# K^T and V^T by transposing DMAs in place of TensorE transposes, in an attention and GLU training step on one core

## The chip, the cores and the metric

The kernel runs on one core of a Trainium2 chip. The metric is the device time of one execution in microseconds (us). A core has TensorE (PE; its weight loads are shown as PEld), VectorE (DVE), ScalarE (ACT), GpSimd (POOL) and SyncE (SP), which work side by side and wait for one another by semaphores; DMA engines move data for the queues that SP and POOL issue.

## What is computed

The reference is a forward pass and its gradients for eight inputs. With S = 2048 rows, D = 576, H = 32 heads of 128 and F = 4608, all in bf16:

```python
xn = layernorm(x)
s  = attention(xn @ wq, k_cache, v_cache) @ wo   # 32 heads, softmax over 2048 keys
g  = silu(glu(xn, w_gate, w_up, w_down))         # (sigmoid(xn@w_gate) * (xn@w_up)) @ w_down
out = x + s * g
# out, and the gradients for x, k_cache, v_cache, wq, wo, w_gate, w_up, w_down
```

## The kernel before, in words

The kernel goes through stages: layer norm and the GLU forward (up to about 510 us of the profile), attention forward and backward for 32 heads (513 to 3774 us), and then the output, the GLU's gradients and the gradient for x. The change lies in the attention stage alone.

**One head.** K and V of a head come from DRAM as natural tiles Kn and Vn, 128 partitions x 16 blocks x 128 (L390, L392, queue of POOL; Kn has two buffers, Vn one). The head's Q^T and dO^T are projections on TensorE. The score matmuls need K^T, and the dP matmuls V^T, each 128 x 2048: TensorE transposes the 16 blocks of Kn, and of Vn, in two groups of eight into PSUM (L431), and VectorE copies each group to KT or VT (L42). KT and VT have one buffer each. For each of the 16 query tiles (128 rows) the first half of the head makes the scores (L465), their scaled negative with a running minimum on VectorE (sneg, L467), the exponentials Pq on ScalarE (L476), and P^T by a transposing DMA of SP (PT, L513), from which TensorE sums the output row by row with Vn (L525). The second half makes dP (L495), dS on VectorE and ScalarE (dSq, L498 to L505), dS^T by a transposing DMA (dST, L513; for query tile 9 alone by TensorE), and dQ rows with Kn (L525). The gradients for V and K (L544) take Pq and dSq as they are, and run beside the rows of the same and of the next head.

**The order is written by hand.** Every piece of a head has a position on a scale of 64 per head: query tile qt has its scores at 2 qt and 2 qt + 1, its dP at 32 + 2 qt and 33 + 2 qt. The other pieces are given with `at(position, function, ...)`: PT is issued at 2 qt + 2.7, dST at 32 + 2 qt + 2.0, the rows are summed from 12.1 positions after the scores (or dP) on. `back(x)` is position x of the head before. K^T of the next head stands at 46.3 and 48.3 of this head, V^T at 22.2 and 24.2 of its own. All entries are sorted by position and called in that order. Inside `tc.manual_schedule(engines=MAN)` the engines of MAN (PE, DVE, ACT) run in the order in which the code calls them; for the others, SP and POOL, a scheduler sets the order. In either case an engine works through its own list in order, so an instruction that waits holds up those behind it.

SP's list in this stage: 16 PT and 15 dST per head, 31 transposing DMAs of 128 x 2048 bf16 (512 KB), and in the last head five loads of Wo into tiles that are no longer needed (L374) and then the loads of oT for the next stage (L694). PT and dST share a pool of seven buffers; Pq and dSq share one of twenty.

Of the kernel before, what the change touches and what calls it, by code (L numbers as in the profile page):

```python
# [9 lines left out]
bf = mybir.dt.bfloat16  # L10
# [3 lines left out]
P = 128  # L14
# [81 lines left out]
def kernel(  # L96
# [6 lines left out]
    nc = tc.nc  # L103
    cfg = dict(cfg or {})
    _, S, D = A_x.shape
# [232 lines left out]
    with tc.tile_pool(name="ld2", bufs=2) as ld2, tc.tile_pool(name="ld1q", bufs=1) as ld1q, \  # L338
# [17 lines left out]
        def at(pos, fn, *args):  # L356
            prog.append((pos, len(prog), fn, args))

        def anchor(pos, fn, *args):
            anchors.append((pos, len(anchors), fn, args))  # L360
# [67 lines left out]
        def pe_transposes(src_fn, dst, g, eng):  # L428
            pt = ps_acc.tile([P, 8, P], bf, name="acct", tag="acc")
            for j in range(8):  # L430
                nc.tensor.transpose(pt[:, j, :], src_fn(g * 8 + j), ident[:])  # L431
            alt.copy(dst[:, g * 8:(g + 1) * 8, :], pt[:], eng=eng)

        def prep_kt(hs, g, eng):
            if g == 0:
                hs.KT = ld1.tile([P, S], bf, name="KT")
            pe_transposes(lambda j: hs.Kn[:, j, :], hs.KT[:].rearrange("p (t q) -> p t q", q=P), g, eng)

        def prep_vt(hs, g, eng):
            if g == 0:  # L440
                hs.VT = ld1.tile([P, S], bf, name="VT")
            pe_transposes(lambda j: hs.Vn[:, j, :], hs.VT[:].rearrange("p (t q) -> p t q", q=P), g, eng)

        def prep_don(hs, g, eng):
            if g == 0:
# [84 lines left out]
        def rows(pos, step, width, hs, T, rhs, g, sinks):  # L530
            bx = Box()
            sink, after = sinks
            for j in range(GQ):
                for kt in range(NT):
                    at(pos + step * j + width * kt / NT, row_mm, bx, hs, T, rhs, g * GQ + j, kt, sink)
            if after:
                at(pos + step * (GQ - 1) + width + AFTER, after)
# [11 lines left out]
        def kv(pos, end, hs, slabs, rhs, half, out_dram):  # L549
            ov = out_dram.rearrange("(p t) d -> p t d", t=NT)  # L550
            bx = Box()
            bx.acc = [None, None]

            def sink(acc, i):
                c = half * 2 + i
                kv_t = stg.tile([P, KPC, P], bf, name="kv")
                alt.copy(kv_t[:], acc[:], eng=KVE[i])
                nc.gpsimd.dma_start(ov[:, c * KPC:(c + 1) * KPC, :], kv_t[:])

            n = 2 * KPC  # L560
            for qt in range(NT):
                for j in range(n):
                    at(pos + (end - pos) * (qt * n + j) / (NT * n), kv_mm, bx, hs, slabs, rhs, half, qt, j, sink)

        def o_sink(hs, g):
            gs = slice(g * GQ, (g + 1) * GQ)
            bx = Box()

            def sink(acc):
                bx.ou = wt.tile([P, GQ, P], bf, name="ou")  # L570
                alt.copy(bx.ou[:], acc[:], eng=OUE)
                bx.prod = wt.tile([P, GQ, P], f32, name="prod", bufs=1)
                nc.gpsimd.tensor_tensor(bx.prod[:], bx.ou[:], hs.dOn[:, gs, :], op=ALU.mult)

            def after():
                prod, ou = bx.prod, bx.ou
                o_n = stg.tile([P, GQ, P], bf, name="o_n", bufs=1)
                nc.vector.tensor_reduce(hs.delta[:, gs], prod[:], axis=AX.X, op=ALU.add)
                nc.gpsimd.tensor_scalar(hs.negdelta[:, gs], hs.delta[:, gs], -1.0, None, op0=ALU.mult)
                nc.gpsimd.tensor_tensor(o_n[:], ou[:], bcast(hs.rinv_all[:, gs], GQ), op=ALU.mult)  # L580
                nc.gpsimd.dma_start(on2_d[g * CH:(g + 1) * CH, hs.h * P:(hs.h + 1) * P].rearrange("(t p) d -> p t d", p=P), o_n[:])

            return sink, after

        def dq_sink(hs, g):
            gs = slice(g * GQ, (g + 1) * GQ)

            def sink(acc):
                dq_n = stg.tile([P, GQ, P], bf, name="dq_n")
                nc.vector.tensor_tensor(dq_n[:], acc[:], bcast(hs.rsc[:, gs], GQ), op=ALU.mult)  # L590
                nc.gpsimd.dma_start(dq2_d[g * CH:(g + 1) * CH, hs.h * P:(hs.h + 1) * P].rearrange("(t p) d -> p t d", p=P), dq_n[:])  # L591

            return sink, None
# [3 lines left out]
        XO, XQ = 12.1, 12.1  # L597
        VA, VB, KA, KB = (22, 38.0), (38.5, 53.5), (58.0, 69.5), (70.5, 82.0)
        QP, DO, KVE, PJE, OUE = (41.0, 3.0), (4.0, 2.5), "ss", "sv", "s"
        KT_AT, DON_AT, VT_AT, QN_AT = (46.3, 2, "v"), (7.2, 5, "v"), (22.2, 2, "v"), (38.3, 2, "s")  # L600
        EXP_AT, RINV_AT, PT_AT, DST_AT, AFTER = 2.1, 4.6, 2.7, 2.0, 3.5
        WO_AT = 50.0
        MAN = {mybir.EngineType.PE, mybir.EngineType.DVE, mybir.EngineType.Activation}
        for h in range(H):
            hs = Head(h)
            b = h * HEAD
            back = lambda x: b - HEAD + x if h else b - 14 + x / 8
            at(back(35.0), load_w, hs)
            at(back(35.1), load_kv, hs)
            for c in range(NCH):  # L610
                at(back(QP[0] + QP[1] * c), proj, hs, "QT", c, PJE[0])
                at(b + DO[0] + DO[1] * c, proj, hs, "dOT", c, PJE[1])
            at(b + DO[0] - 2, prep_wo, hs, "s")
            for g in range(2):
                at(back(KT_AT[0] + KT_AT[1] * g), prep_kt, hs, g, KT_AT[2])
                at(b + DON_AT[0] + DON_AT[1] * g, prep_don, hs, g, DON_AT[2])
                at(b + VT_AT[0] + VT_AT[1] * g, prep_vt, hs, g, VT_AT[2])
                at(b + QN_AT[0] + QN_AT[1] * g, prep_qn, hs, g, QN_AT[2])
            for p in range(NT // 2):
                at(b + 4 * p + 2 + RINV_AT, s_rinv, hs, p)  # L620
                at(b + max(4 * p + 2.1 + RINV_AT, DON_AT[0] + DON_AT[1] * (p // 4) + 0.5), s_scale, hs, p)
            for qt in range(NT):
                p1, p2 = b + 2 * qt, b + H1 + 2 * qt
                for hf in range(NHF):
                    anchor(p1 + hf, s_half, hs, qt, hf)
                    anchor(p2 + hf, dp_half, hs, qt, hf)
                at(p1 + EXP_AT, s_exp, hs, qt)
                if qt in PE_P:
                    for g in range(2):
                        at(p1 + 5.3 + g, trans_pe, hs.PT, hs.P, qt, "PT", g, "s")  # L630
                else:
                    at(p1 + PT_AT, trans_dma, hs.PT, hs.P, qt, "PT")
                if qt in PE_DS:
                    for g in range(2):
                        at(p2 + 4.3 + g, trans_pe, hs.dST, hs.dS, qt, "dST", g, "sv"[g])
                else:
                    at(p2 + DST_AT, trans_dma, hs.dST, hs.dS, qt, "dST")
            for g in range(NG):
                rows(b + 8 * g + XO, 2, 2, hs, hs.PT, "Vn", g, o_sink(hs, g))
                rows(b + H1 + 8 * g + XQ, 2, 2, hs, hs.dST, "Kn", g, dq_sink(hs, g))  # L640
            for half, (pv, pk_) in enumerate(((VA, KA), (VB, KB))):
                kv(b + pv[0], b + pv[1], hs, hs.P, "dOn", half, out_3[0, h])
                kv(b + pk_[0], b + pk_[1], hs, hs.dS, "Qn", half, out_2[0, h])
# [4 lines left out]
                at(bl + WO_AT + 3 * k, load_wo, h0, min(h1, H - 1))  # L648
        prog.sort(key=lambda e: e[:2])
        anchors.sort(key=lambda e: e[:2])  # L650
        with tc.manual_schedule(engines=MAN):
            nxt = 0
            for (pos, _, fn, args) in prog:
                while nxt < len(anchors) and anchors[nxt][0] <= pos:
                    anchors[nxt][2](*anchors[nxt][3])
                    nxt += 1
                fn(*args)

    OB = 5
    if True:  # L660
# [19 lines left out]
        with tc.tile_pool(name="c1b", bufs=1, side="right", reuse_waits="tile") as blk, \  # L680
# [3 lines left out]
                tc.tile_pool(name="c1pt", bufs=2, space=PSUM) as pst, \  # L684
                tc.manual_schedule(engines=MAN | {mybir.EngineType.SP, mybir.EngineType.Pool}):
            gins = {}
# [188 lines left out]
        with tc.tile_pool(name="c4c", bufs=1, reuse_waits="tile") as chp, tc.tile_pool(name="c4s", bufs=2, reuse_waits="tile") as sb, \  # L875
# [10 lines left out]
            for sbi in range(S // SB2):  # L886
# [20 lines left out]
                for sl in range(nsl):  # L907
# [17 lines left out]
                    t = sb.tile([P, D], f32, name="t")  # L925
# [38 lines left out]
```

## Time and profile before

| | |
|---|---|
| median of three runs (lowest, highest) | 5231.35 us (5222.84, 5238.27) |
| span of the profiled execution | 5231.1 us |
| attention, first to last head's score start (31 heads) | 517.3 to 3640.0 us, 100.7 us a head |
| TensorE, share of the span | 97%, mean granted clock 0.996 |
| VectorE, ScalarE, GpSimd | 62%, 44%, 28% |
| copies PSUM to KT, 64 | 691 ns each |
| copies PSUM to VT, 64 | 686 ns each |
| transposing DMAs PT and dST | 512 and 480, median 5.9 us from issue to landing |

The profile is one execution. A page of it has the busy time of each engine, the span in 40 slices with the busy share in tenths, the DMA queues, the chain of work that ended last, and the groups of instructions with busy time, mean duration, idle time before them and what ended it. A matmul's duration runs from issue to the modelled end of a pipeline, so neighbouring matmuls overlap, and the pace is read from the starts. A slice of SP's queue holds the wait of the instruction as well as its issue; the transfer itself comes after it, up to the landing.

### The profile page before, as it was taken

What the parts mean: (1) busy time and instruction counts of PE and PEld (TensorE: products, weight loads), DVE (VectorE), ACT (ScalarE), POOL (GpSimd) and SP (SyncE); (2) the same over time, 40 slices, a digit from 0 to 9 for tenths busy, and PEclk for the clock granted to TensorE, in tenths of its full rate; (3) what the DMA queues carried; (4) which work ended last, traced back from release to release, by engine and by line L of the source; (5) the groups of instructions that cost most, each with busy time, mean ns of one, the idle gap of its engine ahead of it and who ended that gap; (6) DMA issues with size and microseconds to landing.
All of it is one profiled execution on the core that took longest, in us unless ns stands there. A gap on an engine that the chain in (4) does not pass through costs nothing.

```text
span 5231.1 us, 128038 instructions
## 1 busy us (share of the span) xinstructions
PE 5100.0 (97%) x55184; PEld 3649.0 (70%) x55184; DVE 3262.9 (62%) x5108; ACT 2290.1 (44%) x2931; POOL 1444.3 (28%) x2102
## 2 busy tenths in 40 slices
PE   8999999999999999999999999999899999999999
PEld 3444777777777777777777777777657788744454
DVE  4545888888888888888888888888532222210111
ACT  6531665565566556556556655655301221100000
POOL 2222233233233323323323332332222222211000
PEclk9999999999999999999999999999999999999999
DMA  7489999999999999999999999999999556686765
GB/s 274 183 205 166 190 192 199 193 197 194 193 197 198 198 198 199 199 197 195 197 202 198 194 201 199 197 197 201 204 223 227 174 169 185 200 232 152 162 146 124
DMA packets 2712232, 1013.46 MB, mean 194 GB/s; under 512 B 2525296, under 2 KB 2645872, under 8 KB 2711664
## 3 DMA queue, kind: packets, MB, share of 16 engines
q1 hardware_dynamic: 2628256, 726.57, 80.8%
q0 software_dynamic: 83408, 278.71, 17.9%
q8 instruction: 431, 7.06, 0.6%
q14 instruction: 137, 1.12, 0.1%
HBM read 172.54 MB, written 201.00 MB: 71 GB/s over the span
## 4 chain that ended last, share of the span: by engine, by line
PE 81%; issue 6%; DVE 6%; DMA 5%; POOL 1%; SPq 1%; ACT 0%; DVEq 0%; POOLq 0%; ACTq 0%
PE acckv L544 15%; PE acc L525 14%; PE dp L495 8%; PE acc L905 7%; PE sp L465 6%; PE accw L807 6%; DVE sneg L467 4%; PE accp L424 4%; PE dh L781 3%; PE acc L306 3%; PE accd L795 3%; PE accq L863 3%; PE acc L854 2%; PE acct L431 2%; PE acc L723 2%
## 5 line engine op out<-in xcount | busy, mean ns | idle before, releaser
L476 ACT ACTIVATE Pq<-sneg,nm 128x2048 bf16<-128x2048 bf16 x512 | 1024.5, 2001 | 389.2 <-DVE sneg L467 386.1
L525 PE MATMUL acc<-Kn,dST 128*128 128x128 bf16 x8192 | 1066.6, 219 | 22.5 <-DMA dST<-dSq 22.4
L525 PE MATMUL acc<-Vn,PT 128*128 128x128 bf16 x8192 | 1022.4, 219 | 10.7 <-DMA PT<-Pq 10.7
L544 PE MATMUL acckv<-dOn,Pq 128*128 128x128 bf16 x8192 | 1031.7, 219 | 0.0
L498 DVE SCALAR_TENSOR_TENSOR dSq<-dp,delta,Pq 128x1024 bf16<-128x1024 f32 x608 | 773.6, 1281 | 349.9 <-PE dp L495 347.6
L544 PE MATMUL acckv<-Qn,dSq 128*128 128x128 bf16 x8192 | 896.2, 219 | 0.0
L544 PEld LDWEIGHTS <-Pq 128*128 128x128 bf16 x8192 | 793.3, 98 | 117.1 <-issue 0.3
L525 PEld LDWEIGHTS <-PT 128*128 128x128 bf16 x8192 | 765.8, 98 | 153.2 <-DMA PT<-Pq 14.2
L525 PEld LDWEIGHTS <-dST 128*128 128x128 bf16 x8192 | 759.0, 98 | 158.1 <-DMA dST<-dSq 28.8
L544 PEld LDWEIGHTS <-dSq 128*128 128x128 bf16 x8192 | 719.0, 98 | 99.8 <-issue 0.3
L467 DVE TENSOR_SCALAR_CACHE_REDUCE sneg<-sp,nm 128x1024 bf16<-128x1024 f32 x512 | 656.5, 1282 | 82.0 <-PE sp L465 56.5
L467 DVE TENSOR_SCALAR_CACHE_REDUCE sneg<-sp 128x1024 bf16<-128x1024 f32 x512 | 625.0, 1221 | 59.5 <-PE sp L465 51.2
L501 ACT ACTIVATE t<-dp,negdelta 128x1024 bf16<-128x1024 f32 x416 | 463.6, 1114 | 420.1 <-PE dp L495 363.2
L465 PE MATMUL sp<-KT,QT 128*128 128x512 bf16 x2048 | 609.2, 379 | 32.5 <-DVE sneg L467 25.4
L495 PE MATMUL dp<-VT,dOT 128*128 128x512 bf16 x2048 | 609.5, 379 | 0.3 <-DVE dSq L498 0.3
L484 POOL TENSOR_TENSOR dOn<-dOn,rinv_all 128x256 bf16<-128x256 bf16 x256 | 155.9, 609 | 658.0 <-DVE rinv_all L480 540.9
L505 DVE TENSOR_TENSOR dSq<-t,Pq 128x1024 bf16<-128x1024 bf16 x416 | 319.0, 767 | 0.0
L807 PEld LDWEIGHTS <-xn_all 128*128 128x128 bf16 (+1 forms) x2880 | 282.7, 100 | 38.6 <-issue 11.1
L905 PEld LDWEIGHTS <-cf 128*128 128x128 bf16 x2304 | 146.0, 98 | 141.7 <-DMA cf<-dg_d 3.6
L918 DVE SCALAR_TENSOR_TENSOR junk<-dxn,xn_all 128x576 f32<-128x576 f32 x16 | 12.1, 758 | 370.3 <-ACT dxn L913 370.3
L591 POOL DMA_DIRECT2D dq_d<-dq_n x128 | 98.6, 770 | 471.9 <-DVE dq_n L590 463.5
L465 PEld LDWEIGHTS <-QT 128*128 128x128 bf16 x2048 | 163.3, 98 | 53.1 <-issue 51.7
(173 smaller groups left out, 6956.1 us busy)
## 6 DMA issues: line engine op xcount, KB each, us to landing
out_dram<-kv POOLq DMA_DIRECT2D x256, 128.0 KB, 4.8
h_d<-h_row POOLq DMA_DIRECT2D x48, 384.0 KB, 2.7
a_d<-a_row POOLq DMA_DIRECT2D x48, 384.0 KB, 2.6
b_d<-b_row POOLq DMA_DIRECT2D x48, 384.0 KB, 3.2
a_blk<-a_d SPq DMA_DIRECT2D x18, 1024.0 KB, 5.8
b_blk<-b_d SPq DMA_DIRECT2D x18, 1024.0 KB, 21.3
du_d<-du_blk POOLq DMA_DIRECT2D x18, 1024.0 KB, 8.5
dg_d<-dg_blk POOLq DMA_DIRECT2D x18, 1024.0 KB, 11.5
```

The costliest lines, as they stand in the source:

```text
L424: nc.tensor.matmul(acc[:], lhsT=w[:, i, :], rhs=srcT[:, i, cs], start=(i == 0), stop=False)
L465: nc.tensor.matmul(sp[:, c * CH:(c + 1) * CH], lhsT=hs.QT[:, qs], rhs=hs.KT[:, hf * HW_ + c * CH: hf * HW_ + (c + 1) * CH], start=True, st ...
L467: nc.vector.tensor_scalar(sneg[:, hf * HW_:(hf + 1) * HW_], sp[:], -SCALE, None if hf == 0 else nm[:, hf - 1:hf], op0=ALU.mult, op1=ALU.mi ...
L476: nc.scalar.activation(Pq[:], sneg[:], AF.Exp, bias=nm[:, hf:hf + 1], scale=-1.0, accum_out=hs.rs_all[:, qt:qt + 1])
L495: nc.tensor.matmul(dp[:, c * CH:(c + 1) * CH], lhsT=hs.dOT[:, qs], rhs=hs.VT[:, hf * HW_ + c * CH: hf * HW_ + (c + 1) * CH], start=True, s ...
L498: nc.vector.scalar_tensor_tensor(dSq[:, hsl], dp[:], hs.delta[:, qt:qt + 1], Pq[:, hsl], op0=ALU.subtract, op1=ALU.mult)
L501: nc.scalar.activation(t[:], dp[:], AF.Identity, bias=hs.negdelta[:, qt:qt + 1], scale=1.0)
L505: nc.vector.tensor_tensor(dSq[:, hsl], t[:], Pq[:, hsl], op=ALU.mult)
L525: nc.tensor.matmul(bx.acc[:, j, :], lhsT=T[qt][:, kt, :], rhs=getattr(hs, rhs)[:, kt, :], start=(kt == 0), stop=(kt == NT - 1))
L544: nc.tensor.matmul(bx.acc[i][:, jj, :], lhsT=slabs[qt][:, k0:k0 + P], rhs=getattr(hs, rhs)[:, qt, :], start=(qt == 0 and jj == 0), stop=(q ...
L807: nc.tensor.matmul(acc[:kd, :FB], lhsT=xn_all[:, st, d0:d0 + kd], rhs=blk_[:, st, :], start=(st == 0), stop=(st == NT - 1))
L905: nc.tensor.matmul(accs[sl][j][:, :nn], lhsT=ch[:, kk, sl * P:(sl + 1) * P], rhs=w_[:, n0:n0 + nn], start=(pi == 0 and kk == 0), stop=(las ...
```

## The change

The eight-block groups of TensorE transposes of Kn and Vn with their copies (`prep_kt`, `prep_vt`) are replaced by one transposing DMA each, issued by SP from the natural tile (`turn`). V^T moves from positions 22.2 and 24.2 to 5.6 of its head, K^T from 46.3 and 48.3 to 52.4 of the head before. SP joins the engines that run in the written order in this stage.

```diff
-        def prep_kt(hs, g, eng):
-            if g == 0:
-                hs.KT = ld1.tile([P, S], bf, name="KT")
-            pe_transposes(lambda j: hs.Kn[:, j, :], hs.KT[:].rearrange("p (t q) -> p t q", q=P), g, eng)
-
-        def prep_vt(hs, g, eng):
-            if g == 0:
-                hs.VT = ld1.tile([P, S], bf, name="VT")
-            pe_transposes(lambda j: hs.Vn[:, j, :], hs.VT[:].rearrange("p (t q) -> p t q", q=P), g, eng)
+        def turn(hs, name, src):
+            t_ = ld1.tile([P, S], bf, name=name)
+            setattr(hs, name, t_)
+            nc.sync.dma_start_transpose(t_[:].rearrange("p (t q) -> p t q", q=P), src(hs).rearrange("p t d -> p (t d)"))
...
-        KT_AT, DON_AT, VT_AT, QN_AT = (46.3, 2, "v"), (7.2, 5, "v"), (22.2, 2, "v"), (38.3, 2, "s")
+        KT_AT, DON_AT, VT_AT, QN_AT = 52.4, (7.2, 5, "v"), 5.6, (38.3, 2, "s")
...
         MAN = {mybir.EngineType.PE, mybir.EngineType.DVE, mybir.EngineType.Activation}
+        MANH = MAN | {mybir.EngineType.SP}
...
+            at(b + VT_AT, turn, hs, "VT", lambda hs: hs.Vn[:])
+            at(back(KT_AT), turn, hs, "KT", lambda hs: hs.Kn[:])
             for g in range(2):
-                at(back(KT_AT[0] + KT_AT[1] * g), prep_kt, hs, g, KT_AT[2])
                 at(b + DON_AT[0] + DON_AT[1] * g, prep_don, hs, g, DON_AT[2])
-                at(b + VT_AT[0] + VT_AT[1] * g, prep_vt, hs, g, VT_AT[2])
...
-        with tc.manual_schedule(engines=MAN):
+        with tc.manual_schedule(engines=MANH):
```

## The prediction

> **What bounds the kernel now.** I read the page first (busy time, the 40 slices), then one head of the attention stage by itself (windows, TensorE's groups, the chain), then TensorE's waits over 26 heads, then the SP queue and the DMA.
>
> ```profile
> PE 5100.0 (97%) x55184; PEld 3649.0 (70%) x55184; DVE 3262.9 (62%) x5108; ACT 2290.1 (44%) x2931; POOL 1444.3 (28%) x2102
> PEclk9999999999999999999999999999999999999999
> DMA  7489999999999999999999999999999556686765
> ```
>
> TensorE (PE) is busy 97% of the span at the full granted clock, but so are the DMA engines in nearly every slice of the attention stage (slices 4 to 29), and the change moves work from the first to the second. "Busy" is no proof of a bound for either, so I take one head: its first score matmul (L465) starts at 2032.0 us, the next head's at 2132.6, so a head is 100.6 us. Its two halves, then TensorE's waits between 1000 and 3600 us (25.8 heads):
>
> ```profile
> 2032.00:2082.20 50.20, 49.00 (x630) 38.59 (x627) 45.17 (x80) 33.05 (x36) 14.36 (x22) 1.00 1.15 197
> 2082.20:2132.60 50.40, 50.40 (x656) 40.03 (x654) 39.38 (x47) 26.52 (x30) 18.36 (x25) 1.00 1.16 203
> ```
>
> ```profile
> PE sp L465 <- DVE sneg L467: 17.2, 51, 0.4
> PE acc L525 <- DMA dST<-dSq: 9.7, 10, 1.6
> PE acct L431 <- DVE dq_n L590: 5.8, 26, 0.2
> PE acc L525 <- DMA PT<-Pq: 1.7, 5, 0.8
> ```
>
> The columns of a window are length, busy time of PE, PEld, DVE, ACT, POOL, clock, DMA share, GB/s. TensorE idles 1.2 us in the first half and not at all in the second; all its waits in 2600 us are 34.4 us. So **attention runs at TensorE's pace**, and what leaves its list shortens the head by its own length, unless something else is nearly as long. VectorE is: 45.2 of 50.2 us in the first half, and the chain of this head runs through it there (L467, 2065 to 2075 us). The DMA share of 1.15 means that packets overlap, so it doesn't tell how full the engines are.
>
> **The change, part by part.**
>
> *TensorE loses 32 transposes a head.* The chain of this head shows what eight cost when nothing waits:
>
> ```profile
> 2045.10 0.45 PE acct L431 x8
> 2110.55 0.45 PE acct L431 x8
> ```
>
> 0.45 us for eight is 56 ns each (the row's "219 ns" is a pipelined duration, three of which overlap). Four groups a head: 1.8 us. 32 heads: 128 x 0.45 = **57.6 us off**. Beside the row: the Trainium skill, "VectorE: DVE Perf Modes", section "The three transpose paths", gives 390 ns for such a block on TensorE and 1309 ns by DMA, and its rule is to use TensorE where a PSUM destination will do, so it speaks against this change. By its figure 1024 transposes would free an estimated 399 us of TensorE; the trace has a seventh of that.
>
> *VectorE loses four copies a head.* The row of VT's copies has 686 ns, that of KT's 691: 1.37 + 1.38 = 2.75 us a head. In the second half VectorE is off the path (39.4 of 50.4). In the first half the two V^T copies stand at positions 22 and 24 of the head's 64 (1.57 us each, so 2066 to 2071 us), where the chain is on VectorE. There it loses 1.37 us against TensorE's 0.9, 0.47 us more slack a head. The waits of the scores for sneg are put down by their place in the head from TensorE's starts: 22 us of lost time over all 32 heads fall on the score tiles 11 to 13, behind these copies. 0.47 x 32 = 15 us is the most that VectorE's lead can recover, 0 the least; I take **12 us off**, near the top because chain and waits are both at this place.
>
> *The SP queue gets two transposes a head,* 33 for 31, of the same shape (128 x 2048, 512 KB) as PT and dST. Both inputs are in SBUF long before: Kn has landed by position 19 or so of the head before its own, Vn by position 50. K^T is written at 52.4, where dST of tile 9 is missing from the queue (TensorE makes that one), and needed at 64, 18 us later. V^T is written at 5.6 and needed at 32, 41 us later. Landing takes 5.9 us in the median, so neither is waited for itself. What counts is what queues behind each.
>
> ```profile
> 2040.79 50.02 SPq L513 DMA_TRANSPOSE PT<-Pq  x16
> ```
>
> ```profile
> SPq L513 <- PE dp L495: 18.0, 8, 3.7
> SPq L513 <- ACT Pq L476: 16.9, 8, 5.4
> SPq L513 <- PE accp L425: 10.5, 3, 4.6
> SPq L513 <- ACT t L501: 5.8, 2, 2.9
> ```
>
> SP's row is solid, 16 transposes in 50.0 us, 3.13 us each. But a slice holds its wait: in this head SP's waits for producers (the four largest are shown) sum to 73.5 of the 100.6 us. 27.1 us are its own, for 32 transposes 0.85 us; the shortest slice is 1.32. Behind V^T stand PT 2 to 15, behind K^T the dST of tiles 10 to 15. I took from the trace the time between each tile's landing and its first matmul at L525 (heads between 1000 and 3500 us): 7.9 to 9.3 us in the median for PT 2 and 3, and 5.4 for PT 5, before which SP waits 4 us anyway; 3.4 us (least 2.1) for dST 10, before which SP waits 2.1. So 1.3 to 2 us of issue is swallowed. The transfer is not quite: alone a tile's packets take 1.85 us (524,288 bytes at 284 GB/s), in company some 2.7, and transposing packets run in 89% of the time. Some landings slip by up to 2.7 us, and dST 7 and 8 have 0.5 and 1.2 us of slack now (they gain 0.7 and 1.4 us from the K^T copies that go). Bounds for all 64: 0, since more traffic speeds nothing up, and 64 x 3.13 = 200 us if each pushes the whole queue by SP's present pace. I take the end that the slacks point to: TensorE's DMA waits outside the last head (14 us by the waits view, 19 by the gaps between starts) grow by half, **10 us on**.
>
> *Written order on SP.* The order of PT and dST in the heads is as before. Only the last head differs: its five loads of Wo (L374, 4.3 MB) stood among PT 2 to 6, and a load of oT (L694) ahead of the last dST, which waited behind it. Now the loads stand among dST 8 to 15, and oT behind them all. TensorE's waits there:
>
> ```profile
> PE acc L525 <- DMA dST<-dSq: 10.3, 3, 6.4
> PE acc L525 <- DMA PT<-Pq: 9.0, 4, 3.6
> ```
>
> Of 19.3 us, the 9.0 and the 6.4 (the last dST) go. New: 4.3 MB take some 17 us (1.15 MB land in 6.4 us, of which about 2 are latency), beside 7 transposes of 1.85 us in 22 us, so the dST are up to 9 us late against slacks of 3.4 to 7.6. Between 0 and 10 us of new waits; I take 5, the middle: 15.4 - 5 = **10 us off**. The first head: Kn lands at 507.8, K^T by 514, the first scores start at 517.3 now: 0.
>
> **Sum.** -57.6 - 12 + 10 - 10 = -69.6. The profiled span is 5231.1 us, and the median of the three runs is 5231.35, the same to 0.3 us. 5231.1 - 69.6 = 5161.5, **5161 us**.
>
> **The rivals.**
> 1. *SP's queue or the transposing DMA is the pace* (slower). 31 transposes fill a head without a gap in SP's row; if 3.13 us is the pace of the pipe, 33 need 2 x 3.13 = 6.3 us more a head: 5231 + 32 x 6.3 = **5432**. It decides as soon as a transpose costs over 98.8 / 33 = 2.99 us by itself. For it: the solid row, 89% of the time with transposing packets, long bursts at 2.7 to 3.2 us a tile. Against: 73.5 us of SP's time are waits for producers, TensorE hardly waits for DMA, and the packets average 161 GB/s with 290 reached in half-microseconds. **0.08.** It is the rule of the Trainium skill, "Perfetto Trace Analysis", section "What 'DMA-bound' means": a sequencer track of solid DMA slices is a bound by itself. Here the waits inside the slices speak against it.
> 2. *The K^T half gives nothing:* dST 7 and 8, with their small slack, come no earlier though TensorE does, and its 0.9 us, 28.8 us over 32 heads, turn into waits at L525: 5161.5 + 28.8 = **5190**. For it: dST 7 is the row with most steady waits (11 us). Against: VectorE loses more there than TensorE. **0.11.**
> 3. *Contention eats it:* each of 64 transposes makes TensorE wait 1.2 us on average, 57.6 + 12 + 10 = 80 us, two fifths of the upper bound: **5231**, no change. For it: lows of 0.05 us in the slack of several PT. **0.06.**
> 4. That the change doesn't do what it says is excluded: the instruction order has 1024 transposes and 128 copies less, 64 transposing DMAs more, the rest of TensorE's, ScalarE's and GpSimd's order unchanged.
>
> **How the numbers follow.** The forecast has 0.75. A measurement tells about 0.3% (16 us) from no change, so faster means under 5215.7: forecast and rival 2, 0.86; within: 0.06; slower: 0.08. Range: down to 5125 (the 57.6, all of VectorE's 15, all 19.3 of the tail and some 14 of the steady waits), up to 5216, which takes in rival 2 and leaves out rivals 1 and 3, 0.14, with the 200 us bound in them.
>
> **What would show it.** Right: heads of 98 to 99 us; 26 heads' TensorE waits for DMA under 25 us; scores' waits for sneg down by half; in the last head under 10 us of DMA waits. Wrong: L525 waiting for PT or dST in each head (contention, with slips behind V^T or K^T), SP's waits for producers gone to nothing (rival 1), or heads of 100 us with dST 7 and 8 late (rival 2).

## The result, and the profile after

| | before | after |
|---|---|---|
| median (lowest, highest) of four runs each | 5234.81 us (5222.84, 5265.43) | 5384.27 us (5355.13, 5391.35) |
| span of the profiled execution | 5231.1 us | 5389.5 us |
| a head, mean of 31 score starts | 100.7 us | 105.3 us |

The change makes the kernel slower: ratio 1.0263, 95% interval 1.0217 to 1.0309, where 0.987 was forecast. It lies outside the range, on the side of rival 1.

The page of after, the same lines as were shown of before, with the first line of its chain:

```profile
PE 5090.6 (94%) x54160; PEld 3601.7 (67%) x54160; DVE 3189.3 (59%) x4980; ACT 2293.6 (43%) x2931; POOL 1447.9 (27%) x2102
PEclk8999999999999999999999999999999999999999
DMA  7576999999999999999999999999999555596865
PE 67%; DMA 21%; issue 5%; DVE 3%; SPq 2%; POOL 1%; ACT 1%; POOLq 0%; DVEq 0%; ACTq 0%
```

The 1024 transposes and 128 copies are gone as counted. Yet the busy share of TensorE fell from 97 to 94%, the mean granted clock from 0.996 to 0.987, and the chain, which had 81% on TensorE and 5% on DMA before, has 67 and 21% now. One head of after (2198.9 to 2306.9 us, 108.0 us, one of the longer ones), as a window:

```profile
2198.90:2306.90 108.00, 100.37 (x1249) 77.55 (x1247) 82.64 (x120) 59.60 (x66) 32.80 (x46) 0.98 1.16 199
```

The DMA moved 199 GB/s, which is what it moved in before's head (197 and 203): more bytes a head, at the same rate, in more time. That is a first sign that the DMA side sets the pace. TensorE's waits of after between 1000 and 3600 us (24.7 heads):

```profile
PE acc L520 <- DMA PT<-Pq: 77.6, 87, 2.9
PE acc L520 <- DMA dST<-dSq: 63.9, 46, 3.7
PE sp L460 <- DVE sneg L462: 7.7, 24, 0.4
PE acct L431 <- DVE dq_n L585: 5.3, 24, 0.2
```

Waits for PT and dST were 11.4 us in the same stretch of before and are 141.5. They are spread over all tiles, 133 waits in 25 heads. The chain of this head names the transfers in which it stands longest:

```profile
2220.15 9.48 DMA PT<-Pq
...
2271.36 9.28 DMA dST<-dSq
...
2287.98 8.76 DMA dST<-dSq
```

And SP's queue through it (start, length, count):

```profile
2211.15 7.45 SPq L508 DMA_TRANSPOSE PT<-Pq  x2
2218.65 1.39 SPq L437 DMA_TRANSPOSE VT<-Vn  x1
2220.15 43.13 SPq L508 DMA_TRANSPOSE PT<-Pq  x14
2263.38 32.73 SPq L508 DMA_TRANSPOSE dST<-dSq  x9
2296.16 1.93 SPq L437 DMA_TRANSPOSE KT<-Kn  x1
```

V^T and K^T stand as planned and their own slices are short. A row of this view joins the neighbouring slices of one kind whatever lies between them, so the gaps have to be taken from the single slices. Between 1000 and 3500 us the longest gap in after is 0.43 us: SP pushes one transpose behind the other, and so through the whole head. Before has 37 gaps of over 0.5 us there, 46 us in all or 1.9 us a head, and each ends 0.03 us after ScalarE was done with the tile that SP turns next.

### The profile page after: what moved, and what is told of

It reads as the page before. It is cut to its first block, busy times and chain, and to the rows that moved or that the text cites. A ratio compares the mean times of both kernels' runs of the same rounds, so it can differ in the third digit from the quotient of the medians.

```text
span 5389.5 us, 126046 instructions
## 1 busy us (share of the span) xinstructions
PE 5090.6 (94%) x54160; PEld 3601.7 (67%) x54160; DVE 3189.3 (59%) x4980; ACT 2293.6 (43%) x2931; POOL 1447.9 (27%) x2102
## 4 chain that ended last, share of the span: by engine, by line
PE 67%; DMA 21%; issue 5%; DVE 3%; SPq 2%; POOL 1%; ACT 1%; POOLq 0%; DVEq 0%; ACTq 0%
PE acckv L539 12%; DMA PT<-Pq 12%; PE acc L520 11%; DMA dST<-dSq 8%; PE acc L901 7%; PE accw L803 5%; PE dp L490 5%; PE sp L460 5%; PE accp L424 4%; PE acc L306 3%; PE accq L859 3%; PE dh L777 3%; DVE sneg L462 2%; PE acc L850 2%; PE acc L719 2%
## 5 line engine op out<-in xcount | busy, mean ns | idle before, releaser
L539 PE MATMUL acckv<-Qn,dSq 128*128 128x128 bf16 x8192 | 914.5, 221 | 0.0
L553 POOL DMA_DIRECT2D out_dram<-kv x256 | 141.3, 555 | 213.3 <-ACT kv L40 205.5
```

The lines of the kernel that those rows point to most:

```text
L539: nc.tensor.matmul(bx.acc[i][:, jj, :], lhsT=slabs[qt][:, k0:k0 + P], rhs=getattr(hs, rhs)[:, qt, :], start=(qt == 0 and jj == 0), stop=(q ...
```

## What SP's slices hold

The prediction read 73.5 of the 100.6 us of SP's slices as waits for producers. One slice of before shows what that reading is worth. The waits view between 2055 and 2063 us, the slice itself, and ScalarE's exponentials of tiles 5 and 6:

```profile
SPq L513 <- ACT Pq L476: 5.4, 1, 5.4
```

```profile
2055.97 5.70 SPq L513 DMA_TRANSPOSE PT<-Pq  x1
```

```profile
2053.85 2.00 ACT L476 ACTIVATE Pq<-sneg,nm 128x2048 bf16<-128x2048 bf16 x1 [2.03 <-DVE sneg L467]
...
2058.74 2.00 ACT L476 ACTIVATE Pq<-sneg,nm 128x2048 bf16<-128x2048 bf16 x1 [2.80 <-DVE sneg L467]
```

The slice is PT of tile 5. Its input was done at 2055.85, 0.12 us before the slice began, so the slice holds no wait for it. SP did wait for this tile, but ahead of the slice, in a gap of 0.6 us. The view's "5.4 us for Pq" ends at 2060.8, when tile 6 was done: an update of the same engine's semaphore that falls into the slice, and that this transpose doesn't need. I then took every PT and dST between 1000 and 3500 us and compared its slice's start with the end of its own producer and with the last matmul on the buffer that it takes over. In none of before's 769 and after's 732 does either lie behind the start. The data was ready earlier by 3.3 us in the median in before, by 7.9 us in after. So a wait for a producer shows as a gap between slices, and not inside a slice, as the text ahead of the prediction has it. Nor does the view tell the two kernels apart: in after's head above its waits still sum to 77.8 of 108.0 us, though the queue has no gap.

So the 3.08 us of a mean slice (3.09 in after) hold no wait for data: they are the price of a transpose in this traffic. What it is spent on shows in the landings: the slice of a transpose ends, in the median, 0.1 to 0.2 us after the landing of the one ahead of it, and half of them between 0.3 us before and 0.5 us after. SP gets rid of a transpose as fast as the one ahead drains. With 0.10 us between slices, before needs 31 x 3.185 = 98.7 us of its 100.7, after 33 x 3.197 = 105.5 of the 105.5 that its heads take in this stretch. **Before had 2.0 us a head left on this queue, and the change asked for 6.4.**

## The experiments

The theory: SP's transposes and the engines that drain them are one pipe with a price per byte, TensorE and this pipe run side by side, and the longer one sets the head. Rivals: the written order; the place of V^T and K^T in the queue; a price per instruction on SP. Each ratio is against before on the same chip; heads are means of the profiled execution. The last column has the gaps of over 0.5 us between SP's slices (1000 to 3500 us, a head).

| kernel | transposing DMAs a head | ratio (95% interval) | head, us | gaps of SP, us |
|---|---|---|---|---|
| before | 31 | 1 | 100.7 | 1.9 |
| after | 33 | 1.0263 (1.0217, 1.0309) | 105.3 | 0 |
| e1_order | 31 | 1.0007 (0.9989, 1.0024) | 100.9 | 1.1 |
| e2_v_only | 32 | 1.0140 (1.0111, 1.0169) | 103.9 | 0.1 |
| e3_ds3 | 31 | 1.0037 (1.0018, 1.0056) | 101.7 | 1.5 |
| e4_no_store | 33, 1 MB of stores less | 1.0047 (1.0025, 1.0069) | 102.0 | 0 |
| e5_half | 31 + 2 halves | 1.0152 (1.0132, 1.0171) | 103.5 | 0 |
| e6_split | 31 + 4 halves | 1.0338 (1.0313, 1.0362) | 106.4 | 0 |
| e7_before_no_store | 31, 1 MB of stores less | 0.9930 (0.9906, 0.9954) | 100.2 | 9.5 |
| e8_dma34 | 34 | 1.0451 (1.0406, 1.0496) | 107.9 | 0 |
| e9_place | 33 | 1.0314 (1.0264, 1.0365) | 105.9 | 1.6 |
| e10_dma30 | 30 | 1.0077 (1.0053, 1.0100) | 102.3 | 13.2 |

Where the queue has next to no gaps left (after, e2, e4, e5, e6, e8) it sets the head; where gaps remain, the head stays within 1.6 us of before's. e9_place alone fits neither.

**e1_order, the written order alone.** Of before:

```diff
-        with tc.manual_schedule(engines=MAN):
+        with tc.manual_schedule(engines=MAN | {mybir.EngineType.SP}):
```

> The kernel before with SP in the written order and nothing else changed. Theory (the 16 DMA engines are full: SP pushes the next transposing DMA only as fast as the last one drains, so a head costs 31 or 33 times about 3.1 us): no transposing DMA is added, so 5215 to 5245 us, as before; the waits of the last head go from 19 us to under 12. Rival (the written order of SP is what costs, by holding up ready transposes behind waiting ones): 5340 us or more.

No change that can be measured. The order is not the cause. Nor does it repair the last head: its waits for PT and dST are 14.8 us, 19.3 before, and not under 12, for the loads of Wo now stand among dST; and those for oT behind them are 8.8 us, 4.5 before.

**e2_v_only, one of the two.** K^T goes back to TensorE (`prep_kt` at 46.3 and 48.3), V^T stays on the DMA.

> V^T by the transposing DMA at 5.6, K^T by TensorE as before: 32 transposing DMAs a head. Theory (DMA engines full, price per transposing DMA the same wherever it stands): half of the loss, 5290 to 5330 us, heads of 102 to 103 us. Rival (place: the loss comes from what queues behind one of the two): about 5235 if it is behind K^T, where the rows of dS tile 7 wait most, about 5380 if behind V^T.

1.0140, half of the loss, with heads of 103.9 us, 0.9 above those expected. Neither place carries it alone.

**e3_ds3, the number back to 31.** Of after:

```diff
-    PE_DS = {9}
+    PE_DS = {4, 9, 14}
```

> The kernel after with dS tiles 4 and 14 transposed by TensorE as well as tile 9: 31 transposing DMAs a head, as many as before, while K^T and V^T stay on the DMA. TensorE has as many transposes as before. Theory (number of transposing DMAs decides): 5210 to 5250 us, heads of 100 to 101 us. Rival (place of K^T and V^T in the queue): 5350 us or more. Rival (written order): 5340 or more.

The median, 5266 us, is above the stated 5250, but so was before on that chip (5250 us); the ratio is 1.0037, and the heads are 101.7 us where 100 to 101 were expected. With V^T and K^T by DMA, where they were, and two other transposes taken out, six sevenths of the loss are gone: the number counts. TensorE's waits that stay, in 26 heads, are 10.2 us of the transposes for a PSUM buffer that ScalarE still empties, and 13.9 us for PT.

**e4_no_store and e7_before_no_store, less of the other traffic.** After and before, without the stores of two gradients from GpSimd's queue for heads 1 to 31.

```diff
-                nc.gpsimd.dma_start(ov[:, c * KPC:(c + 1) * KPC, :], kv_t[:])
+                if hs.h == 0:
+                    nc.gpsimd.dma_start(ov[:, c * KPC:(c + 1) * KPC, :], kv_t[:])
```

> The kernel after without the stores of the gradients for k_cache and v_cache of heads 1 to 31 (those outputs are left out): 1 MB less a head for the DMA engines, the 33 transposing DMAs as they are. Theory (the engines' throughput is the bound; in the trace a SP slice grows by 4.4 ns for each KB that GpSimd's queue moves beside it): 1024 KB x 4.4 ns = 4.5 us a head, 31 heads, so 5230 to 5270 us, down to TensorE's pace. Rival (SP's issue of the transposing instruction is the pace, whatever else the engines move): 5370 to 5390 us, unchanged.

> The kernel before without the stores of the gradients for k_cache and v_cache of heads 1 to 31 (left out). Theory (31 transposes fit beside TensorE with a few us to spare, so before runs at TensorE's pace): no more than its few waits for DMA go, 0.993 to 1.000 of before, heads of 100.3 us. Rival (before was already at the pace of the DMA engines): 4 us a head less, 0.975.

In after, 1 MB less on another queue takes 3.3 us off each head, with all 33 transposes in place: four fifths of the loss by the ratio. So a slice isn't SP's time alone; it is shared with what else the engines move. The theory gave 4.5 us; a quarter of it didn't come (the median is 5274 us, just over the range), and the reason is not shown. The queue has no gap yet, with 33 slices of 2.99 us where after has 3.09, and the waits of e4_no_store in the same stretch show that it is still the DMA that TensorE waits for:

```profile
PE acc L520 <- DMA PT<-Pq: 59.5, 71, 2.5
PE acc L520 <- DMA dST<-dSq: 17.0, 26, 1.5
```

In before the same MB takes off 0.5 us a head, its few DMA waits; the median head is 100.3 us, and SP's gaps grow to 9.5 us a head. This is TensorE's own pace: before was bound by TensorE, as predicted, but with the other bound 2 us behind.

**e5_half and e6_split, bytes or instructions.** In e5_half the DMA turns blocks 8 to 15 of both, TensorE the others. In e6_split each of the two DMAs is cut into two of 128 x 1024, which is the diff:

```diff
-            nc.sync.dma_start_transpose(t_[:].rearrange("p (t q) -> p t q", q=P), src(hs).rearrange("p t d -> p (t d)"))
+            for g in range(2):
+                nc.sync.dma_start_transpose(t_[:].rearrange("p (t q) -> p t q", q=P)[:, g * 8:(g + 1) * 8, :], src(hs)[:, g * 8:(g + 1) * 8, :].rearrange("p t d -> p (t d)"))
```

> The kernel after with only blocks 8 to 15 of K^T and V^T by transposing DMA (128 x 1024) and blocks 0 to 7 by TensorE and VectorE as before: 33 transposing instructions a head, bytes of 32. Theory (price per byte): about as V^T alone by DMA, 1.012 to 1.017 of before. Rival (price per instruction on SP): as the kernel after, 1.026 or more.

> The kernel after with K^T and V^T each in two transposing DMAs of 128 x 1024: 35 instructions a head, the bytes of 33. Theory (price per byte): as the kernel after, 1.024 to 1.030 of before. Rival (price per instruction): two more slices of about 3.1 us a head, 1.05 to 1.065.

Two halves cost as much as one whole (1.0152, and 1.0140 in e2_v_only). Four halves in place of two wholes cost 1.1 us a head more, 0.55 us for each instruction, not a slice of 3.1. The price is for the bytes, with a small part for the instruction; 1.0338 lies between the two expectations, nearer to the first.

**m1_bench, the transpose by itself.** Its core, called once for each group with the count and the columns:

```python
for k in range(n):
    t_ = wp.tile([P, cols // P, P], bf, name=name, tag="W" if cols <= 2048 else "W2", bufs=7 if cols <= 2048 else 4)
    nc.sync.dma_start_transpose(t_[:], src[:, 0:cols])
```

> No part of the computation: only transposing DMAs of one SBUF tile, back to back on SP, in five groups: 24 of 128 x 2048 alone; 24 beside matmuls; 24 beside 16 stores of 128 KB from GpSimd's queue; 48 of 128 x 1024; 12 of 128 x 4096. Theory (engines drain 512 KB in 1.8 us at best, other traffic and SBUF use slow them): 1.8 to 2.0 us each alone, 2.3 to 2.6 beside matmuls or beside stores, half the time for half the size, twice for twice. Rival (SP's issue has a price per instruction): 2.5 us alone, the same beside stores, 1.3 us or more for the half size.

Its timeline of SP, from its one execution (start, length, count): alone, beside matmuls, beside stores, half size, double size.

```profile
4.21 58.97 SPq L113 DMA_TRANSPOSE alone<-src  x24
63.22 61.25 SPq L113 DMA_TRANSPOSE beside_pe<-src  x24
124.52 68.40 SPq L113 DMA_TRANSPOSE beside_st<-src  x24
193.37 66.17 SPq L113 DMA_TRANSPOSE half<-src  x48
259.58 59.48 SPq L113 DMA_TRANSPOSE twice<-src  x12
```

With nothing beside it, waiting for nothing, 512 KB take 58.97 / 24 = 2.46 us, where the prediction had 1.85; the double size takes 4.96 and the half 1.38. Matmuls beside it add 0.1 us in the mean, through two slices of 3.6 and 3.9 us; the other 22 are as they are alone. 16 stores of 128 KB add 9.4 us to their group, 4.6 ns for each KB. The slope over the slices of before and after is much the same: a line fitted through them gives 4.7 and 4.5 ns for each KB that GpSimd's queue moves beside them, on 2.59 and 2.64 us without any. A head moves some 3,440 KB on that queue: with 2.6 us and 4.5 ns, 33 x 2.6 + 3440 x 4.5 ns + 33 x 0.1 = 105 us, and 99 for 31. The 1.9 us alone of the theory is refuted as much as the unchanged time beside stores of the rival, whose 2.5 us alone came true.

**e8_dma34, one more.** Tile 9's dST by DMA as well (`PE_DS = set()` in after), TensorE 0.9 us a head less.

> The kernel after with dS tile 9 by DMA too: 34 transposing DMAs a head, TensorE 0.9 us a head less. Theory (DMA engines full, each 128 x 2048 transpose costs 3.1 to 3.2 us of their time in this mixture): 1.043 to 1.050 of before, heads of 108 to 109 us. Rival (the loss is waits at certain places of the queue that one more transpose need not lengthen): 1.015 to 1.030.

1.0451, with heads of 107.9 us, just under those expected. From 31 to 34 the steps of the ratio are 1.4, 1.2 and 1.9%, 2.0 to 3.1 us a transpose, though TensorE has less to do at each.

**e9_place, elsewhere in the queue.** In after, `KT_AT` 38.9 in place of 52.4, `VT_AT` 19.7 in place of 5.6.

> The kernel after with V^T written at 19.7 in place of 5.6 and K^T at 38.9 in place of 52.4. Theory (price per byte on full engines): the place doesn't matter, 1.022 to 1.031 of before. Rival (what queues behind them at 5.6 and 52.4 has too little slack): more than half of the loss gone, or far more lost, outside 1.015 to 1.040.

1.0314, with an interval that overlaps after's and reaches over the upper end stated, 1.031. SP waits 1.6 us a head here, ahead of a PT, and the head is 105.9 us all the same: this place is no better, and of what it costs by itself no run tells.

**e10_dma30, one fewer than before.** `PE_DS = {4, 9}` in before.

> The kernel before with dS tile 4 by TensorE as well as tile 9: 30 transposing DMAs a head, 16 more TensorE transposes. Theory (before is at TensorE's pace, with the DMA engines only a few per cent under it): 0.9 us a head more for TensorE, up to 0.4 us of DMA waits less, 1.002 to 1.008. Rival (before was already held by the DMA engines): 0.98.

Slower, 1.0077, as expected at its upper end: TensorE has 0.9 us more, and the added transposes wait for PSUM buffers (23 us in 26 heads). Before stands where the two bounds meet; none of the versions that leave nothing out beats it.

## Why the prediction was wrong

*TensorE's 57.6 us:* right, though nearly four transposes overlap (219 ns at a start every 56 ns), not three. The gaps between matmul starts beyond their usual pace grew by 6.4 us a head, and the head by 4.6: the 1.8 us are there, paid over. A part of the 6.4 is the clock: in after's attention stage it is granted at half for 14 stretches, 51 us in all, in before's for one of 3.4 us. That is at most 26 us of TensorE's time, 0.8 us a head. Nine of the 14 begin within 2.5 us of a wait of over 2 us, and before has no wait as long; so the waits probably bring them, but no run separates the two.

*The SP queue's two transposes,* the step that failed. The prediction took SP's slices for waits ("27.1 us are its own, for 32 transposes 0.85 us") and let the added ones vanish in them, at 10 us for all 64. The runs show slices without a wait in them, 3.1 us each, on a queue with 2.0 us a head to spare. The term is 64 x 3.2 = 205 us of the pipe's time, of which 2.0 us x 32 = 64 found room: 141 us, where the ratio gives 138. The upper bound, 200 us, was the nearest row; the prediction named it and went to the other end. The two signs that it argued away, a solid row of SP and transposing packets in 89% of the time, could not have settled it: e7_before_no_store, whose queue stands empty for 9.5 us a head, has a row just as solid, and transposing packets ran in 91% of its time against 92% of before's (1000 to 3500 us).

```profile
2023.16 52.07 SPq L513 DMA_TRANSPOSE PT<-Pq  x16
```

What would have settled it is the 1.9 us of gaps a head, less than two of the shortest slices (1.32 us each).

*Rival 1* is what happened. Its 5432 us came out too high by 48 since it let before's pipe be full; it had 2.0 us of slack a head (64 us) there. Its threshold, 2.99 us for a transpose, was right, and 3.2 is over it. Its sign, SP's waits for producers gone to nothing, did not come (77.8 us by the view), because what the view gives are no waits in either kernel. The rule that it quoted, of the Trainium skill ("Perfetto Trace Analysis", section "What 'DMA-bound' means"), that a sequencer track of solid DMA slices is a bound, agrees with the trace of after, with no gap over 0.43 us. That section puts such slices down to the generation of descriptors and not to the movement of data; there the runs differ, since the stores of another queue lengthen them (9.4 us in m1_bench).

*Rival 3* had the waits, but at 1.2 us for a transpose; the time lost was 6.4 x 32 / 64 = 3.2. The slack of dST 7, on which *rival 2* rested, fell from 0.5 to 0.05 us, but so did that of PT 5, so it was not K^T's half alone.

*The slacks behind V^T and K^T* were measured rightly but for PT 2 and 3 (9.0 and 9.3 us), and meant little. They hold off a delay that is made good later. A queue that is longer than the head makes nothing good, and each tile came later until its slack was gone: PT 5 landed 5.4 us ahead of its use in before's median, 0.05 in after's.

*VectorE's 12 us:* the scores' waits for sneg fell by more than half, as said, and it was worth nothing, since TensorE waited elsewhere. *The last head's 10 us:* not there; 18.8 us of waits for PT and dST in after, 19.3 before, and e1_order gave the order alone no gain. Only the 4.5 us of waits for oT behind them are gone.

## What to carry to other kernels

An engine at 97% is only the first bound; before work is moved off it, the second must be known in the same unit, as time that the receiving queue really has left in a head (here 2.0 us for two transposes of 3.2). Whether a queue is full is read from the gaps between its single slices, not from a row that joins them. Slices that stand back to back mean a full queue until each one's own producer is shown to end inside it; a view that names a releaser by the nearest semaphore update doesn't show that. And a price for a transfer is taken from a stretch that lasts, with the usual traffic beside it, not from the fastest burst.

## What the hardware showed unasked

A transposing DMA from SBUF to SBUF of 128 x 2048 bf16 has a steady pace of 2.46 us (213 GB/s) with nothing beside it, though half-microseconds of 290 GB/s occur in the kernel. Size hardly helps (4.96 us for twice, 1.38 for half). Ordinary stores from another queue slow it nearly one for one: the 2.1 MB of m1_bench's stores would take 9.8 us at 213 GB/s, and their group took 9.4 us longer. While their packets ran (131.3 to 145.2 us) the transposes fell to 83 GB/s and the stores moved 150, a sum of 233. Which part sets the 2.46 us, the engines' handling of 256-byte packets (64.11 MB in 250,416) or SP's feeding of them, no run here tells; that other traffic takes its share of the same time is shown, and is why stores of another queue are paid for in TensorE's waits.
